# Channel attention and a gated MLP on one core: v's first half split two steps later, turned weights made in three pieces, block 1's v turned within block 0, last block ended by output halves

## The chip, the cores and the metric

The kernel runs on one core of a Trainium2 chip. The metric is device time in microseconds (us). An execution repeats within some 0.1%: the three runs of the kernel before lie between 1318.31 and 1320.58 us.

The engines have two names each: PE is TensorE's matrix product and PEld its weight load, DVE is VectorE, ACT is ScalarE, POOL is GpSimd, SP is SyncE, which here only issues transfers (DMAs).

## The reference

Inputs are q, k and v (2 x 6016 x 256), the weights w_gate, w_val (256 x 1536) and w_out (1536 x 256), and scales, all in fp32.

```python
def _attn_ref(q, k, v, tau):
    qn = q / (np.linalg.norm(q, axis=1, keepdims=True) + 1e-06)
    kn = k / (np.linalg.norm(k, axis=1, keepdims=True) + 1e-06)
    s = kn.transpose(0, 2, 1) @ qn / tau          # 256 x 256 per batch
    ...
    return v @ a                                  # a: softmax of s over its last axis

def _moe_ref(x, w_gate, w_val, w_out, rms_g):
    xn = x / np.sqrt(np.mean(x * x, axis=-1, keepdims=True) + 1e-06) * rms_g
    g = xn @ w_gate
    return (g / (1 + np.exp(-g)) * (xn @ w_val)) @ w_out
```

The attention's output, taken as 12032 rows, is x of the second function.

## The kernel before, in words

**Precision.** Every operand of a large product is split into a high part (a ScalarE copy to a rounded type) and a low part (a subtraction on VectorE or GpSimd). A product is then three matmuls: high by high, high by low, low by high. So each tensor that TensorE reads costs one ScalarE copy and one subtraction, and those have to be done in time.

**Blocks and steps.** The rows of v are cut into 24 blocks of 512 rows (the first and the last of 384). A block has 12 steps, one for each 128 columns f of the hidden layer. (j, f) is step f of block j. Blocks 0 and 1 use plain products (`emit_hidden`, L776 on), with the score products of batch 1 filled in between. From block 2 on, `emit_step` (L710 on) forms the hidden layer with seven products of quarter blocks in place of eight, in a flight of three steps: a step begins with products 7 and 2 of the step that started two steps earlier, continues with products 3 and 6 of the one in the middle, then 5 and 1 of the new one, and ends with product 4 of the oldest, with output products before and behind product 4. `new_state` gives each step one of three PSUM banks with tag u. ScalarE copies products out to t (L739, L744), VectorE adds them (L732, L733), ScalarE applies silu in even steps (L748, L766), VectorE multiplies in odd steps (L751, L760).

**Output.** In odd steps `round_pair` puts down the splits of a finished pair p (p = 0 to 5, steps 2p and 2p+1): first gx (copy L665, subtraction L671 on GpSimd), and in the next odd step gy and, for pairs 2 to 4 from block 4 on (the Strassen pairs), gz. Between the two, in the even step, `run_turned` (L657) forms differences in place in zg, with four VectorE instructions that wait for GpSimd to have read gx's part. The output products of a step (L860) run five steps later. The Strassen pairs need weights s, so, which `build_so` makes in block 3 and 4 in two pieces: piece 0 forms sums on VectorE (L595, L605), piece 1 copies on ScalarE (L611) and subtracts on VectorE (L613). `build_s` does the like for the hidden layer's weights in blocks 1 and 2. Their scratch wk has one buffer, which `post_out`'s sums also use.

**The next x.** While a block's steps run, x of later blocks is made: `load_v`, `move_v` (VectorE transposes into vw, L406; one buffer), `split_v` (ScalarE L390, then L391 on GpSimd, on VectorE for blocks 0 and 1), `emit_x` (TensorE px, L428), `emit_x_squares`, `emit_rr` (GpSimd) and `emit_xn` (ScalarE L469), `emit_xT_move` (VectorE L504, and after its second half 16 transfers on SP, L513), `emit_xT_scale` (ScalarE L523), `emit_xT_parts` (GpSimd L534, L539) and `emit_xT_round` (ScalarE L551, GpSimd L553). Blocks 0 and 1 turn v and x on TensorE instead (`turn_v`, `emit_xT_first`).

**What sets the order.** The order is written out by hand in tables that say which of these parts follows which step: turn0 to turn4 for blocks 0 to 4 and steady for all later ones; their values run behind a step, those of the _mid tables within it and those of the _pre tables before the silu. `of(m, go)` runs go for block j+m. In the tables v0 and v1 are move_v of the two halves, s0 and s1 split_v, x0/q0/r0/n0 and x1/q1/r1/n1 the products, squares, roots and scaling, m0 and m1 the transposes of x, scale, parts, hi and rest what follows. `at(j, f, go)` adds further parts behind a step. Each engine executes its instructions in the order in which they are written. `next_bank` gives blocks 0 and 1 a rotation of four PSUM banks (three of tag u, one of tag q).

The lines that matter most in the tables before:

```python
        steady = {
            1: (scale,),
            3: (hi, v1),
            ...
            11: after(3, vm(0), vs(0)),
        }
```

Of the kernel before, what the change touches and what calls it, by code (L numbers as in the profile page):

```python
# [15 lines left out]
P = 128  # L16
# [3 lines left out]
def kernel(  # L20
# [352 lines left out]

    def turn_v(j, h, psum, tag):

        x = v_t[j].rearrange("p m c r -> p (m c r)")
        v_w[j, h] = psum.tile([P, KC, HN], F32, tag=tag, name=f"pvt_{j}_{h}")
        for c in range(KC):
            for i, t in enumerate(half_tiles(j, h)):
                nc.tensor.transpose(  # L380
                    v_w[j, h][:, c, i * P:(i + 1) * P],
                    x[:, t * C + c * P:t * C + (c + 1) * P], ident,
                )
# [207 lines left out]
    def build_so(k, piece):  # L591
# [14 lines left out]
        else:  # L606
            t = s_tmp.pop(("so", k))[:, 2:].rearrange("p i n -> p (i n)")
            src = (t[:, :3 * P], t[:, 3 * P:])
            hi, lo = ([x[:, k], w[:, 2 * p + 1, P:]] for x, w in zip(so_hl, wo))
            for o, x in zip(hi, src):  # L610
                nc.scalar.activation(out=o, in_=x, func=AF.Copy)  # L611
            for o, x, y in zip(lo, src, hi):
                nc.vector.tensor_tensor(out=o, in0=x, in1=f32(y), op=ALU.subtract)  # L613
# [196 lines left out]
    def out_rows(j):  # L810

        r, mu0 = strided(j)
        return out[r, :].rearrange("(s m) e -> s m e", s=S)[:, mu0:mu0 + A * blocks[j][2], :]
# [32 lines left out]
    def emit_out_turned(j, f):  # L846
# [3 lines left out]
        jobs = G.pop((j, f))  # L850
        todo = [(b, o, w[wi], g[gi], wi + gi) for wis, gi in (((0, 1), 0), ((0,), 1)) for b, o, w, g in jobs for wi in wis]
        half = (len(todo) + 1) // 2

# [44 lines left out]
    def post_store(j):  # L898

        n = blocks[j][2]  # L900
        h = n * P // 2
        w = sums.pop(j)
        ob = v_p.tile([P, A * BT, KC, S], F32, tag="v", name=f"ob_{j}")
        for e in range(2):
            nc.vector.transpose(
                out=ob[:, :A * n, e, :],
                in_=w[:, 2 * e * h:2 * (e + 1) * h].rearrange("p (m s) -> p m s", s=S),
            )
        dst = out_rows(j).rearrange("s m (e i r) -> i s m e r", e=KC, i=A)
        for i in range(A):  # L910
            queue = nc.scalar if i % 2 and j == NB - 1 else nc.sync
            queue.dma_start(
                out=dst[i].rearrange("s m e r -> s (m e) r"),
                in_=ob[S * i:S * (i + 1), :A * n].rearrange("p m e r -> p (m e) r"),
            )
        del o_ps[j]


    with tc.manual_schedule():
# [51 lines left out]
        for h in range(2):  # L971
            turn_v(0, h, ps_gv, "u")
        nc.vector.tensor_scalar(out=mtau, in0=mtau, scalar1=-1.0, scalar2=None, op0=ALU.mult)
# [61 lines left out]
        emit_xT_first(0, 1)  # L1035
        turn_v(1, 0, ps_m, "m")
        add()
# [7 lines left out]
        def at(j, f, go):  # L1045
            extra.setdefault((j, f), []).append(go)
# [41 lines left out]
        at_step = [(2 * p + 2, 2 * p + 3, 2 * p + 4, 2 * p + 4) for p in range(NP - 3)]  # L1088
        at_step += [(8, 9, 10, 12), (13, 14, 15, 16), (16, 18, 19, 20)]
        for i in (2, 3, 0, 1):  # L1090
# [13 lines left out]
        at(STRA - 1, 6, new_so)  # L1104
        for k, (f0, f1) in enumerate(((10, 11), (12, 13), (14, 15))):
            for i, f in enumerate((f0, f1)):
                at(STRA - 1 + f // NF, f % NF, lambda k=k, i=i: build_so(k, i))

# [20 lines left out]
        def vs(h):  # L1129
            return lambda n: split_v(n, h)  # L1130

        def x(h):
            return lambda n: emit_x(n, h)

        def sq(h):
# [8 lines left out]
        def xm(c):  # L1144
            return lambda n: emit_xT_move(n, c)
# [4 lines left out]
        def of(m, go):  # L1150
# [18 lines left out]
        steady = {  # L1169
            1: (scale,),  # L1170
            3: (hi, v1),
# [5 lines left out]
            9: (m0,),  # L1177
            11: after(3, vm(0), vs(0)),
        }
# [3 lines left out]
            **steady,  # L1183
            0: after(1, xm(1)),
            1: (v0, s0),
# [4 lines left out]
        }  # L1190
        turn4_mid = {6: (x0, q0, r0), 8: (x1, q1), 9: (n1,)}
        turn3 = {
            0: after(1, xm(1)),
            3: (v0,),
# [6 lines left out]
            10: (r1,),  # L1201
            11: (m0,),
        }
        turn3_mid = {5: (parts,), 7: (x0, q0, r0), 9: (x1, q1), 11: (n1,)}
        turn2 = {
            **turn3,
            0: after(1, sq(1), rr(1)),
            1: after(1, xn(1), xm(0), xm(1)),
            4: (scale, s0),
# [17 lines left out]
        turn0 = {  # L1227
            0: after(1, vs(0)),
            1: after(1, x(0), sq(0), rr(0)),
            2: after(1, xn(0), lambda n: turn_v(n, 1, ps_m, "m")),  # L1230
            3: after(1, vs(1)),
            4: after(1, x(1), sq(1), rr(1)),
            5: after(1, xn(1)),
            8: (of(1, lambda n: emit_xT_first(n, 0)), v0),
# [36 lines left out]
        post_sums(NB - 1)  # L1271
        for o in owed:
            run = emit_out(*o[1:])
            run(0)
            run(1)
        for e in range(2):
            post_out(NB - 1, e)
        post_store(NB - 1)


# [31 lines left out]
```

## Time and profile before

| | |
|---|---|
| three runs | 1318.31, 1319.4 (median), 1320.58 us |
| the profiled execution | 1320.82 us |
| its span, first to last instruction | 1319.0 us |
| mean granted TensorE clock | 0.993 of 2.4 GHz |
| instructions | 25099, of them 9216 matmuls |

The span lies within the execution; 1.8 us are around it. A matmul's end is modelled, so TensorE's idle time is best read from its waits. A timeline row gives the start, the duration, engine, line, operation, out<-in by the program's names, shape and count, with the idle time of the engine before it and what ended it in brackets.

### The profile page before, as it was taken

Reading aid. Unit: us, or ns where it says so; the run is one execution under the profiler, and the core shown is the slowest. Engines: PE = TensorE matmul, PEld = TensorE weight load, DVE = VectorE, ACT = ScalarE, POOL = GpSimd, SP = SyncE. Lnnn points to the kernel's source line nnn. Section 1 sums busy time; section 2 is a strip of 40 time slices with the busy share of each in tenths; the row PEclk is TensorE's granted clock in tenths of the full one; section 3 lists DMA queues with packets and bytes.
Section 4 is the critical chain, followed back from the end, with each engine's and each line's share of the span. In section 5 each row is a group of like instructions: output and inputs, shape, how many; then the busy total and the mean of one; then the engine's idle time right before and its main releaser. Section 6 shows DMA issues by size and latency. Waiting matters only on the chain.

```text
span 1319.0 us, 25099 instructions
## 1 busy us (share of the span) xinstructions
PE 1274.4 (97%) x9216; PEld 1205.1 (91%) x9216; DVE 965.2 (73%) x1588; ACT 857.3 (65%) x1773; POOL 807.7 (61%) x642
## 2 busy tenths in 40 slices
PE   8989998999999999999999999999999999999997
PEld 7779988998999999999999999999999999999997
DVE  5789687657678767777777777677677687686765
ACT  5566556665766676666666766766766766766653
POOL 0120244765676776776777777777777777776643
PEclk9899999999999999999999999999999999999999
DMA  8868111120211211212202202202202202101101
GB/s 285 286 238 261 40 32 34 22 44 17 43 23 33 40 26 33 37 25 37 33 18 48 33 18 49 33 17 49 33 17 49 34 17 49 29 18 28 17 8 22
DMA packets 226588, 71.77 MB, mean 54 GB/s; under 512 B 189600, under 2 KB 218016, under 8 KB 226464
## 3 DMA queue, kind: packets, MB, share of 16 engines
q1 hardware_dynamic: 224896, 69.97, 23.0%
q8 instruction: 72, 1.18, 0.4%
q14 instruction: 52, 0.43, 0.1%
q10 hardware_dynamic: 1568, 0.20, 0.1%
HBM read 46.40 MB, written 12.32 MB: 45 GB/s over the span
## 4 chain that ended last, share of the span: by engine, by line
PE 53%; DVE 9%; POOL 5%; issue 3%; ACT 2%; SPq 2%; DMA 1%; DVEq 0%; ACTq 0%
PE pu L703 28%; PE po L860 17%; POOL gx L671 5%; PE pq L703 4%; DVE zg L657 4%; PE px L428 4%; ACT gx L665 2%; SPq L513 2%; DVE zg L760 2%; DMA xnT<-xw 1%; DVE zv L732 1%; DVE zg L751 1%; DVE zv L733 0%; DVE zg L732 0%; DVE os L885 0%
## 5 line engine op out<-in xcount | busy, mean ns | idle before, releaser
L703 PE MATMUL pu<-xt,w 128*128 128x256 f32 (+1 forms) x2376 | 415.7, 283 | 18.9 <-DVE zv L732 12.1
L703 PEld LDWEIGHTS pu<-xt,w 128*128 128x128 f32 x2376 | 347.8, 189 | 37.4 <-DVE zv L732 15.7
L703 PE MATMUL pu<-xt,s 128*128 128x256 f32 (+1 forms) x2376 | 372.0, 281 | 3.4 <-ACT t L739 1.4
L703 PEld LDWEIGHTS pu<-xt,s 128*128 128x128 f32 x2376 | 329.0, 189 | 20.0 <-DVE zg L760 5.5
L671 POOL TENSOR_TENSOR gy<-zg,gy 128x512 fp32r<-128x512 f32 (+1 forms) x131 | 170.9, 1305 | 193.7 <-ACT gy L665 160.3
L671 POOL TENSOR_TENSOR gx<-zg,gx 128x512 fp32r<-128x512 f32 (+3 forms) x131 | 202.0, 1542 | 64.4 <-ACT gx L665 55.7
L751 DVE TENSOR_TENSOR zg<-zg,zv 128x768 f32<-128x768 f32 (+1 forms) x132 | 210.8, 1597 | 14.1 <-DVE zv L733 0.5
L744 ACT ACTIVATE t<-pu 128x512 f32<-128x512 f32 (+1 forms) x264 | 156.3, 592 | 87.2 <-PE pu L703 51.0
L860 PE MATMUL po<-gx,w 128*128 128x256 f32 (+3 forms) x972 | 205.2, 330 | 0.7 <-ACT gx L665 0.7
L657 DVE TENSOR_TENSOR zg<-zg 128x256 f32<-128x256 f32 (+1 forms) x240 | 119.5, 498 | 61.8 <-POOL gx L671 55.6
L860 PE MATMUL po<-gy,w 128*128 128x512 f32 (+3 forms) x612 | 163.3, 360 | 0.0
L665 ACT ACTIVATE gx<-zg 128x512 fp32r<-128x512 f32 (+3 forms) x132 | 95.6, 724 | 99.0 <-DVE zg L760 54.8
L860 PEld LDWEIGHTS po<-gx,w 128*128 128x128 f32 x972 | 143.2, 188 | 6.9 <-ACT gx L665 0.8
L732 DVE TENSOR_TENSOR zv<-pu,t 128x512 f32<-128x512 f32 (+1 forms) x132 | 89.8, 680 | 75.7 <-ACT zg L766 36.5
L739 ACT ACTIVATE t<-pu 128x256 f32<-128x256 f32 (+1 forms) x264 | 98.9, 375 | 65.5 <-PE pu L703 64.9
L703 PE MATMUL pq<-xt,w 128*128 128x256 f32 (+1 forms) x792 | 137.2, 281 | 0.0
L732 DVE TENSOR_TENSOR zg<-pu,t 128x512 f32<-128x512 f32 (+1 forms) x132 | 90.3, 684 | 61.3 <-PE pu L703 27.7
L665 ACT ACTIVATE gy<-zg 128x512 fp32r<-128x512 f32 (+1 forms) x132 | 82.7, 626 | 78.6 <-DVE zg L657 63.7
L671 POOL TENSOR_TENSOR gz<-zg,gz 128x512 fp32r<-128x512 f32 (+1 forms) x60 | 118.2, 1969 | 0.0
L703 PEld LDWEIGHTS pq<-xt,w 128*128 128x128 f32 x792 | 112.1, 188 | 0.0
L748 ACT ACTIVATE zg<-zg 128x768 f32<-128x768 f32 (+1 forms) x132 | 109.6, 830 | 0.0
L860 PEld LDWEIGHTS po<-gy,w 128*128 128x128 f32 x612 | 101.1, 188 | 6.2
(138 smaller groups left out, 1977.0 us busy)
## 6 DMA issues: line engine op xcount, KB each, us to landing
v<-in_v_dram SPq DMA_DIRECT2D x84, 128.0 KB, 3.7
xnT<-xw SPq DMA_DIRECT2D x336, 32.0 KB, 1.9
out_dram<-ob SPq DMA_DIRECT2D x84, 128.0 KB, 3.3
raw<-in_q_dram SPq DMA_DIRECT2D x20, 512.0 KB, 5.3
raw<-in_k_dram SPq DMA_DIRECT2D x20, 512.0 KB, 6.5
wraw<-in_moe_w_gate_dram SPq DMA_DIRECT2D x12, 256.0 KB, 3.6
wraw<-in_moe_w_val_dram SPq DMA_DIRECT2D x12, 256.0 KB, 4.1
wraw<-in_moe_w_out_dram SPq DMA_DIRECT2D x12, 256.0 KB, 5.0
```

The source lines that it names most:

```text
L428: nc.tensor.matmul(out=px[:, i, :], lhsT=w[:, c, i * P:(i + 1) * P], rhs=x[:, c, :], start=(i == 0 and c == 0 and m == 0), stop=(c == KC - ...
L513: nc.sync.dma_start(out=x[S * i:S * (i + 1), :, a * n * S:(a + 1) * n * S], in_=w[S * a:S * (a + 1), :, i, :n, :].rearrange("p c t s -> p ...
L657: nc.vector.tensor_tensor(out=z[:, o], in0=z[:, i0], in1=z[:, i1], op=ALU.subtract)
L665: nc.scalar.activation(out=gh, in_=hh, func=AF.Copy)
L671: engine.tensor_tensor(out=gl, in0=hh, in1=f32(gh), op=ALU.subtract)
L703: nc.tensor.matmul(out=out, lhsT=wm[wi], rhs=xm[xi], start=(start and q == 0), stop=(q == 2), skip_group_check=True,)
L732: nc.vector.tensor_tensor(out=z[:, 1:], in0=u, in1=t[:, :2], op=ALU.add)
L739: nc.scalar.activation(out=mt[:, 0], in_=mu[:, 1], func=AF.Copy)
L744: nc.scalar.activation(out=nt[:, 1:], in_=nu, func=AF.Copy)
L748: nc.scalar.activation(out=zg[:, 1:], in_=zg[:, 1:], func=AF.Silu)
L751: nc.vector.tensor_tensor(out=zg[:, 1:], in0=zg[:, 1:], in1=z, op=ALU.mult)
L860: nc.tensor.matmul(out=acc[b][:, o:o + g.shape[-1]], lhsT=w, rhs=g, start=first, stop=True, skip_group_check=True,)
```

## The change

- Steady blocks: the split of v's first half (`split_v`, h = 0) goes from the end of step 11 to the end of step 1 of the next block, ahead of scale. move_v stays at step 11.
- `build_so` has three pieces: sums, copies, subtractions; they stand at steps (3, 8), (3, 11), (4, 0) for the first pair, (4, 0), (4, 1), (4, 2) for the second, (4, 2), (4, 3) and within (4, 4) for the third.
- Block 1's v is turned behind steps 0 and 3 of block 0, into banks of the rotation; split, product and scaling of both halves follow one step later each than before.
- m1 of blocks 4 and 5 goes from step 0 of a block to step 11 of the one before; xn of block 3's second half from (2, 1) to (2, 0); build_s of pair 4 begins at (2, 0) and not (2, 1).
- Last block: the output products of steps 10 and 11 are ordered by output half; each half is summed, transposed and stored by itself, with four transfers on two queues per half in place of four for both.

```diff
-    def turn_v(j, h, psum, tag):
+    def turn_v(j, h):
...
-        v_w[j, h] = psum.tile([P, KC, HN], F32, tag=tag, name=f"pvt_{j}_{h}")
+        v_w[j, h] = next_bank(f"pvt_{j}_{h}").rearrange("p (c n) -> p c n", c=KC)
...
-            t = s_tmp.pop(("so", k))[:, 2:].rearrange("p i n -> p (i n)")
+            t = s_tmp["so", k][:, 2:].rearrange("p i n -> p (i n)")
...
-            for o, x in zip(hi, src):
+            for o, x in zip(hi, src) if piece == 1 else ():
                 nc.scalar.activation(out=o, in_=x, func=AF.Copy)
-            for o, x, y in zip(lo, src, hi):
+            for o, x, y in zip(lo, src, hi) if piece == 2 else ():
                 nc.vector.tensor_tensor(out=o, in0=x, in1=f32(y), op=ALU.subtract)
...
+        if (j, f) >= (NB - 1, NF - 2):
+            todo.sort(key=lambda job: job[0])
...
         for e in range(2):
+            if j == NB - 1:
+                sums[j] = w
+                post_out(j, e)
             nc.vector.transpose(
...
+            if j == NB - 1:
+                dst = out_rows(j)[:, :, e * P:(e + 1) * P].rearrange("s m (i r) -> i s m r", i=A)
+                for i in range(A):
+                    (nc.scalar if i % 2 else nc.sync).dma_start(
+                        out=dst[i], in_=ob[S * i:S * (i + 1), :A * n, e, :]
+                    )
...
-        turn_v(1, 0, ps_m, "m")
...
-        at_step += [(8, 9, 10, 12), (13, 14, 15, 16), (16, 18, 19, 20)]
+        at_step += [(8, 9, 10, 12), (12, 14, 15, 16), (16, 18, 19, 20)]
...
-        for k, (f0, f1) in enumerate(((10, 11), (12, 13), (14, 15))):
-            for i, f in enumerate((f0, f1)):
-                at(STRA - 1 + f // NF, f % NF, lambda k=k, i=i: build_so(k, i))
+        for i, k, f in ((0, 0, 8), (1, 0, 11), (2, 0, 12), (0, 1, 12), (1, 1, 13), (2, 1, 14), (0, 2, 14), (1, 2, 15)):
+            at(STRA - 1 + f // NF, f % NF, lambda k=k, i=i: build_so(k, i))
...
         steady = {
-            1: (scale,),
+            1: (s0, scale),
...
-            11: after(3, vm(0), vs(0)),
+            11: after(3, vm(0)),
...
         turn4 = {
             **steady,
-            0: after(1, xm(1)),
...
-        turn4_mid = {6: (x0, q0, r0), 8: (x1, q1), 9: (n1,)}
+        turn4_mid = {4: (lambda j: build_so(2, 2),), 6: (x0, q0, r0), 8: (x1, q1), 9: (n1,)}
         turn3 = {
-            0: after(1, xm(1)),
...
-            11: (m0,),
+            11: (m0, m1),
...
         turn2 = {
             **turn3,
-            0: after(1, sq(1), rr(1)),
-            1: after(1, xn(1), xm(0), xm(1)),
+            0: after(1, sq(1), rr(1), xn(1)),
+            1: after(1, xm(0), xm(1)),
...
         turn0 = {
-            0: after(1, vs(0)),
-            1: after(1, x(0), sq(0), rr(0)),
-            2: after(1, xn(0), lambda n: turn_v(n, 1, ps_m, "m")),
-            3: after(1, vs(1)),
-            4: after(1, x(1), sq(1), rr(1)),
-            5: after(1, xn(1)),
+            0: after(1, turn(0)),
+            1: after(1, vs(0)),
+            2: after(1, x(0), sq(0), rr(0)),
+            3: after(1, xn(0), turn(1)),
+            4: after(1, vs(1)),
+            5: after(1, x(1), sq(1), rr(1)),
+            6: after(1, xn(1)),
...
-        for o in owed:
-            run = emit_out(*o[1:])
-            run(0)
-            run(1)
-        for e in range(2):
-            post_out(NB - 1, e)
+        owed = [emit_out(*o[1:]) for o in owed]
+        for part in range(2):
+            for go in owed:
+                go(part)
         post_store(NB - 1)
```

## Rows read from the trace of the kernel before

**Rows 1.** The page, part 1: busy us, share of the span, instructions

```profile
PE 1274.4 (97%) x9216; PEld 1205.1 (91%) x9216; DVE 965.2 (73%) x1588; ACT 857.3 (65%) x1773; POOL 807.7 (61%) x642
```

**Rows 2.** TensorE's waits, 340 to 1200 us: by whom; us, times, longest

```profile
PE pu L703 <- DVE zv L732: 12.1, 17, 0.9
```

**Rows 3.** Timeline, VectorE and GpSimd, blocks 17 and 18: start us, us, instruction

```profile
1008.71 1.80 DVE L657 TENSOR_TENSOR zg<-zg 128x256 f32<-128x256 f32 x4 [0.41 <-POOL gx L671]
1016.67 2.88 DVE L657 TENSOR_TENSOR zg<-zg 128x256 f32<-128x256 f32 x4 [1.05 <-POOL gx L671]
1016.59 1.29 POOL L391 TENSOR_TENSOR vt<-vw,vt 128x512 fp32r<-128x512 f32 x1
```

**Rows 4.** Timeline, TensorE entering steps 1 and 3, blocks 18, 22; VectorE

```profile
1016.64 0.52 PE L703 MATMUL pu<-xt,s 128*128 128x256 f32 x3
1025.56 0.51 PE L703 MATMUL pu<-xt,s 128*128 128x256 f32 x3
1215.98 0.52 PE L703 MATMUL pu<-xt,s 128*128 128x256 f32 x3
1223.82 0.51 PE L703 MATMUL pu<-xt,s 128*128 128x256 f32 x3
1216.01 1.80 DVE L657 TENSOR_TENSOR zg<-zg 128x256 f32<-128x256 f32 x4 [1.05 <-POOL gx L671]
```

**Rows 5.** Timeline, ScalarE, GpSimd and VectorE around the new place, block 18

```profile
1014.61 0.62 ACT L390 ACTIVATE vt<-vw 128x512 fp32r<-128x512 f32 x1
1024.33 0.36 ACT L739 ACTIVATE t<-pu 128x256 f32<-128x256 f32 x1
1023.55 1.31 POOL L671 TENSOR_TENSOR gx<-zg,gx 128x512 fp32r<-128x512 f32 x1
1027.03 1.29 POOL L671 TENSOR_TENSOR gy<-zg,gy 128x512 fp32r<-128x512 f32 x1 [2.17 <-ACT gy L665]
1030.36 1.56 POOL L539 TENSOR_TENSOR xp<-xnT,xp 128x256 f32<-128x256 f32 x2
1029.39 0.75 DVE L406 STREAM_TRANSPOSE vw<-v 128x256 f32<-128x256 f32 x2
```

**Rows 6.** Timeline, TensorE's waits around block 0 (idle us and releaser in brackets)

```profile
76.89 0.66 PE L380 MATMUL pvt<-ident,v 128*128 128x128 f32 x4 [1.63 <-DMA v<-in_v_dram]
85.74 2.62 PE L428 MATMUL px<-a,vt 128*128 128x256 f32 x12 [2.24 <-DVE vt L391]
96.81 0.66 PE L380 MATMUL pvt<-ident,v 128*128 128x128 f32 x4 [1.21 <-ACT xn L469]
```

**Rows 7.** Block 0: us; busy PE, PEld, DVE, ACT, POOL; clock; DMA share, GB/s

```profile
77.00:118.40 41.40, 37.95 (x212) 35.42 (x213) 38.01 (x51) 28.27 (x48) 5.58 (x4) 0.96 0.77 232
86.07:89.48 3.41, 3.41 (x16) 3.14 (x15) 3.41 (x6) 2.36 (x8) 0.15 (x1) 0.50 0.14 51
```

**Rows 8.** Timeline, start of block 2: TensorE, GpSimd, ScalarE

```profile
218.14 0.62 PE L703 MATMUL pu<-xt,w 128*128 128x256 f32 x3 [2.21 <-DVE zg L732]
230.84 0.62 PE L703 MATMUL pu<-xt,s 128*128 128x256 f32 x3 [1.39 <-ACT t L739]
211.94 0.72 POOL L457 TENSOR_TENSOR rr<-ss,mhalf 128x2 f32<-128x2 f32 x1
214.08 0.83 ACT L469 ACTIVATE xn<-px,rr 128x256 f32<-128x256 f32 x2
```

**Rows 9.** Timeline, TensorE, blocks 3 and 4

```profile
319.44 0.62 PE L703 MATMUL pu<-xt,w 128*128 128x256 f32 x3 [1.37 <-DVE zg L732]
329.36 0.62 PE L703 MATMUL pu<-xt,w 128*128 128x256 f32 x3 [1.89 <-DVE zg L732]
```

**Rows 10.** Timeline, VectorE and the store's issue at the end

```profile
1311.85 1.02 DVE L894 TENSOR_TENSOR os<-po,os 128x384 f32<-128x384 f32 x2
1313.84 0.89 SPq L912 DMA_DIRECT2D out_dram<-ob  x2
```

**Rows 11.** DMA issues, 1312 to 1320 us: operation xcount, KB each, us to landing

```profile
out_dram<-ob SPq DMA_DIRECT2D x2, 96.0 KB, 3.0
```

More of the change, by code (lines that the diff above doesn't have):

```diff
@@ L908, in post_store @@
             )
+            if j == NB - 1:
[4 more added lines that the diff above has]
+                    )
         dst = out_rows(j).rearrange("s m (e i r) -> i s m e r", e=KC, i=A)
-        for i in range(A):
-            queue = nc.scalar if i % 2 and j == NB - 1 else nc.sync
-            queue.dma_start(
+        for i in range(A if j < NB - 1 else 0):
+            nc.sync.dma_start(
                 out=dst[i].rearrange("s m e r -> s (m e) r"),
@@ L971 @@
         for h in range(2):
-            turn_v(0, h, ps_gv, "u")
+            turn_v(0, h)
         nc.vector.tensor_scalar(out=mtau, in0=mtau, scalar1=-1.0, scalar2=None, op0=ALU.mult)
@@ L1133, in x, with turn @@
             return lambda n: emit_x(n, h)
+        def turn(h):
+            return lambda n: turn_v(n, h)
         def sq(h):
```

## The prediction

> **What bounds the kernel now.** I read the page first: TensorE is busy for 97% of the span, VectorE for 73%, GpSimd for 61% [rows 1]. Such shares are averages, so they only say that an engine that feeds TensorE late costs time, and that nothing else does. Next come TensorE's own waits [rows 2]: from block 4 on one entry stands out, 17 waits of up to 0.9 us for the same VectorE instruction. The count matters: 17 blocks (j = 4 to 20) prepare the v of block j+3 at their step 11. So I read the engines' timelines around one of these waits, at 1016 to 1026 us [rows 3]. The four subtractions of run_turned (L657) take 2.88 us there and 1.80 us one pair earlier. The only thing that differs beside them is GpSimd's subtraction for v's first half (L391, 1.29 us), which starts as they do. The late L657 holds back L732, L732 holds a PSUM bank, and TensorE waits for that bank.
>
> The trace has its own control [rows 4]. Block 21 prepares no v any more (there is no block 24). In step 1 of block 22 L657 takes 1.80 us again, and TensorE has no wait of that kind. From the first product of step 1 to the first of step 3 it needs 1223.82 - 1215.98 = 7.84 us there and 1025.56 - 1016.64 = 8.92 us beside the v work. The difference, 1.08 us, is exactly 2.88 - 1.80. That is the price per block, second-hand delays included.
>
> **Part 1: v's first half split two steps later.** ScalarE's copy and GpSimd's subtraction leave the end of step 11 and go to the end of step 1, ahead of the scaling L523. What is removed: 17 x 1.08 = 18.4 us, all on the path. What the new place costs [rows 5]: on ScalarE the copy (0.62 us) goes in front of L523, behind which the copy L739 queues. L739 ends at 1024.33 + 0.36 = 1024.69; TensorE overwrites what it reads with the first product of step 3, at 1025.56 [rows 4]. Of 0.87 us of slack 0.25 is left: cost nothing, but thin. On GpSimd the subtraction comes right behind gx (1023.55 to 1024.86), and the next thing is gy at 1027.03: 2.17 us are free for 1.29. VectorE's next user of the buffer vw is L406 at 1029.39, long after. No DMA moves. Bounds: nothing lost (18.4), or the copy's whole 0.62 per block on the path (17 x (1.08 - 0.62) = 7.8). I take 18.4, since the slack is measured and the control shows the rest of the chain without further wait.
>
> The Trainium skill, "SBUF — State Buffer", section "Who interferes with whom", says that a VectorE instruction with two SBUF inputs and a GpSimd instruction that reads SBUF exclude each other, the second one blocked until the first is done. By that the whole 1.29 us would be lost and regained, 17 x 1.29 = 21.9 us; the rows give 1.08, and I keep them.
>
> **Part 2: block 1's v turned within block 0.** Before, TensorE waits three times here [rows 6]: 1.63 us for v's load in front of block 0, 2.24 us for VectorE's half of the split, 1.21 us for the PSUM bank m. Together 5.08 us. After the longest its granted clock is 0.50 (1.2 GHz) for 3.41 us [rows 7], which loses half of that, 1.7 us. So 6.8 us are there at most. The change moves the first turn behind step 0 (the load has landed by then), gives both turns banks of the rotation instead of m, and puts one step between turning, splitting and multiplying. But VectorE is nearly full: from 77 to 118.4 us it is busy for 38.01 of 41.40 us, so its stream, which still has to make both splits, can move up by 3.4 us only. TensorE may run ahead of it a little, since it uses weights made two steps earlier. Bounds 3.4 and 6.8; I take 4.1, near VectorE's bound: a shorter wait before each product px remains (about 0.9 and 0.6 us when I lay the two engines' instructions end to end), none of them long enough for the clock to fall, since after the 1.63 us wait it did not fall either. The four transposes per half are moved and not added. Block 0's own turns take the same kind of bank as before: nothing.
>
> **Part 3: start of block 2.** xn(1) of block 3 goes from the end of step 1 to the end of step 0, the first piece of the turned weights of pair 4 likewise. Two waits stand here [rows 8]: 2.21 us for VectorE's L732, queued behind the transposes L504 that wait for xn, and 1.39 us for ScalarE's L739, queued behind a scaling that waits for those transposes' 16 transfers. xn could start once GpSimd's rr is done, at 211.94 + 0.72 = 212.66 instead of 214.08. So transposes, transfers and scaling come 1.4 us earlier, and that is the gain at the second wait, whatever the first becomes. The new order also makes ScalarE wait for rr and delays its copies for TensorE's step 2: I expect a wait of about 1.7 us at the first product of step 2 in place of the 2.21. Bounds 0 and 3.6; I take 1.4.
>
> **Part 4: turned weights in three pieces, and m1 of blocks 4 and 5 one step earlier.** TensorE waits 1.37 and 1.89 us where VectorE's L613 stands in one piece with ScalarE's copies that it needs [rows 9]. With the subtraction a step later VectorE no longer waits for ScalarE, but its work is the same: in steps 0 and 2 of block 4 two pieces now meet (a piece 2 and a piece 0). Of 3.3 us I take 3.0, with 1.5 as the lower end, since VectorE then runs some tenths late. The transposes' 16 transfers are issued on SP about one step earlier, with no other transfer of the loop overtaken; their reader, the scaling, is four steps on: nothing. The earlier transposes add 0.7 us to VectorE in step 11, which step 0 loses.
>
> **Part 5: the end.** VectorE's last four instructions (sums L894 from 1311.85 and transposes L905, up to the issue of the stores at 1313.84: 2.0 us) stay, in the order sum, transpose, sum, transpose; so the first half's four transfers can start about 1.0 us earlier [rows 10]. The last half still starts where all did, but with half the bytes behind it. Landing took 3.0 us for 96 KB [rows 11]. TensorE's reordering only has to finish bank 0 before VectorE gets to L894. I take 1.0 us, bounds 0.3 and 1.5.
>
> The Trainium skill, "DMA: Bandwidth & Descriptors", its table of fixed and variable time, has about 2 us per DMA that do not shrink with size, and only the bytes' own time on top. By that the tail would gain some 0.45 us, as an estimate from that page, in place of 1.0.
>
> **The sum.** 18.4 + 4.1 + 1.4 + 3.0 + 1.0 = 27.9 us. The profiled execution took 1320.82 us (span 1319.0 and 1.8 around it), 1.4 above the median of 1319.4. 1320.82 - 27.9 = 1292.9 there, so 1291.5 for a median run (27.9 off the median). Ends of the terms, not all at once: gains of 22 to 33, 1286 to 1298.
>
> **Rivals.**
> (a) The split finds a new victim. If GpSimd's subtraction slides behind gy of step 3, it stands beside L751, which like L657 reads two SBUF operands, and a wait of the old kind comes back; between nothing and all of the 18.4 us I take half: 27.9 - 9.2 = 18.7, 1300.7. For it: the thin slack on ScalarE. Against: GpSimd executes in program order, and 2.17 us are free in front of gy. 12%. The rule of the Trainium skill's "SBUF — State Buffer", section "Who interferes with whom", allows this case as well as mine.
> (b) Only part 1 and the end pay. In block 0 VectorE is the bound, and the waits of parts 2 to 4 move instead of going: 18.4 + 1.0 = 19.4, 1300.0. For it: 38.01 of 41.40 us. Against: waits of 5.08 us and a fallen clock have to be paid again in places where VectorE has no wait today. 9%.
> (c) The change does not do what it says: L657 is slow for another reason, and part 1 gives nothing: 9.5, 1309.9. Against: the control. 2%.
> (d) Slower. vw is one buffer, and the next thing that VectorE does with it is L406 at 1029.39. If the subtraction ran only behind GpSimd's train of step 3, which ends at 1030.36 + 1.56 = 1031.92 [rows 5], it would end at 1033.2, and L406 would wait 3.8 us with L732 behind it. It decides once the subtraction ends after 1029.39, which is 3.2 us later than the 1026.15 at which it should end. If two thirds of the 3.8 us reach TensorE, 17 x 2.5 = 43 us: 1334. Against: the program order again. 3%.
>
> My forecast has the remaining 74%. The range takes in most of (a) and (b): 1286 to 1300.5. A measurement of this kernel can tell about 0.2%, 2.6 us, from no change. Forecast, (a), (b) and (c) are all faster by more than that; I leave 2% for a mixture that ends within it.
>
> **What would show it.** Right: L657 at 1.8 us in every strassen step, no entry of 17 waits for L732, every block with v work 1.08 us shorter; no granted clock of 0.50 near 86 us; one wait near 216 us, shorter than 2.21; VectorE never waiting for L611; output transfers in two groups, 1 us apart. Wrong: a wait for L739 at step 3's first product, 17 times (part 1's slack was too thin); waits for L391 in block 0 that add up to 5 us (part 2); L732 late in steps 1 to 3 of block 4 (part 4).

## The result, and the profile after

The changed kernel takes 1296.81 us (median of 4 runs, 1295.19 to 1298.8), the kernel before 1319.36 us beside it (median of 4). The ratio is 0.983, with a 95% interval from 0.981 to 0.985. The prediction was 1291.5 us with a range from 1286 to 1300.5, so the sign and the range hold and the middle was 5.3 us too low. The profiled executions differ by 24.9 us (spans 1319.0 and 1294.1), the medians by 22.5, since the execution profiled after was 0.9 us under its median and the one before 1.5 over its own.

The first thing to read is again the page's busy times and TensorE's waits, of the kernel after. Beside [rows 1], TensorE does the same 9216 matmuls and VectorE is busy for 19 us less, though it does the same work.

```profile
PE 1268.4 (98%) x9216; PEld 1202.7 (93%) x9216; DVE 945.9 (73%) x1588; ACT 853.7 (66%) x1773; POOL 806.0 (62%) x642
```

TensorE's waits over the whole span, after (by whom; us in all, times, longest):

```profile
PE s L174 <- DMA raw<-in_k_dram: 5.9, 5, 2.5
PE pu L703 <- ACT t L739: 3.9, 3, 1.8
PE pv L786 <- DVE vt L391: 2.5, 1, 2.5
PE px L428 <- DVE vt L391: 1.6, 1, 1.6
PE pu L703 <- DVE zg L732: 1.3, 1, 1.3
PE pu L703 <- DVE zv L732: 1.3, 2, 1.0
```

The entry of 17 waits for L732 [rows 2] is gone. Where it stood, L657 is as fast in step 1 as in every other step; the group by lines shows it for all 240 instructions (busy us, mean ns), first before and then after:

```profile
L657 DVE TENSOR_TENSOR zg<-zg 128x256 f32<-128x256 f32 (+1 forms) x240 | 119.5, 498 | 61.8 <-POOL gx L671 55.6
L657 DVE TENSOR_TENSOR zg<-zg 128x256 f32<-128x256 f32 (+1 forms) x240 | 101.3, 422 | 61.8 <-POOL gx L671 55.6
```

The timeline of step 1 of one block after, which answers to the late L657 of [rows 3]:

```profile
996.90 1.80 DVE L657 TENSOR_TENSOR zg<-zg 128x256 f32<-128x256 f32 x4 [1.05 <-POOL gx L671]
```

But the list has an entry that the prediction did not have, 2.5 us in one wait of the product pv. Of the three waits for ScalarE's L739 one was forecast, 1.73 us at the first product of step 2 of block 2 ("about 1.7"); the other two, 1.76 and 0.37 us, were not.

**Where the time came from.** The same five matmuls are found in both traces, and the time between them compared. The landmarks are the first product pg of step 11 of block 1, the product 2 (pq) of step 8 of block 2, of step 6 of block 4 and of step 4 of block 21, and the last matmul. Each stretch holds one part of the change. Times in us, from the traces:

| stretch | part | before | after | gain | forecast |
|---|---|---|---|---|---|
| start to block 1, step 11 | 2 | 203.61 | 200.55 | 3.06 | 4.1 |
| to block 2, step 8 | 3 | 36.88 | 36.59 | 0.29 | 1.4 |
| to block 4, step 6 | 4 | 94.46 | 92.00 | 2.46 | 3.0 |
| to block 21, step 4 | 1 | 844.89 | 826.60 | 18.29 | 18.4 |
| to the last matmul | none | 131.52 | 131.73 | -0.21 | 0 |
| to the end | 5 | 7.67 | 6.66 | 1.01 | 1.0 |

Parts 1 and 5 came out as forecast, the other three gave 5.8 us in place of 8.5. The rest of this document asks whether part 1 works for the stated reason, and what took the missing 2.7 us. The last four stretches repeat within about 0.1 us in most executions of the same code, so a single execution is enough to read a part. The first one varies more: the five kernels here with the block 0 of before have 201.57 to 204.54 us, mean 202.8, and seven with that of after 199.04 to 201.78, mean 200.4, so that part 2 is worth 2.5 us over all of them. Experiments for which no interval is given were executed once, and are read by their stretches.

### The profile page after: what moved, and what is told of

The parts are those of the page before. It is cut to its first block, busy times and chain, and to the rows that moved or that the text cites. A ratio compares the mean times of both kernels' runs of the same rounds, so it can differ in the third digit from the quotient of the medians.

```text
span 1294.1 us, 25106 instructions
## 1 busy us (share of the span) xinstructions
PE 1268.4 (98%) x9216; PEld 1202.7 (93%) x9216; DVE 945.9 (73%) x1588; ACT 853.7 (66%) x1773; POOL 806.0 (62%) x642
## 4 chain that ended last, share of the span: by engine, by line
PE 90%; DVE 4%; DMA 2%; issue 1%; SPq 1%; ACT 1%; POOL 1%; DVEq 0%; ACTq 0%; POOLq 0%
PE pu L703 42%; PE po L862 26%; PE pq L703 7%; PE px L428 5%; PE s L174 4%; DMA raw<-in_k_dram 2%; PE po L828 2%; PE pv L786 2%; PE pg L786 2%; SPq L513 1%; DVE wx L122 0%; DVE acc L198 0%; DVE w L137 0%; DVE wo L605 0%; SPq L160 0%
## 5 line engine op out<-in xcount | busy, mean ns | idle before, releaser
L671 POOL TENSOR_TENSOR gy<-zg,gy 128x512 fp32r<-128x512 f32 (+1 forms) x131 | 182.1, 1390 | 176.2 <-ACT gy L665 148.4
L751 DVE TENSOR_TENSOR zg<-zg,zv 128x768 f32<-128x768 f32 (+1 forms) x132 | 202.4, 1533 | 14.1 <-DVE zv L733 0.5
L657 DVE TENSOR_TENSOR zg<-zg 128x256 f32<-128x256 f32 (+1 forms) x240 | 101.3, 422 | 61.8 <-POOL gx L671 55.6
L732 DVE TENSOR_TENSOR zv<-pu,t 128x512 f32<-128x512 f32 (+1 forms) x132 | 89.7, 679 | 74.0 <-ACT zg L766 36.5
L739 ACT ACTIVATE t<-pu 128x256 f32<-128x256 f32 (+1 forms) x264 | 99.0, 375 | 63.9 <-PE pu L703 63.4
L732 DVE TENSOR_TENSOR zg<-pu,t 128x512 f32<-128x512 f32 (+1 forms) x132 | 90.2, 684 | 62.6 <-PE pu L703 27.7
```

The lines of the kernel that those rows point to most:

```text
L657: nc.vector.tensor_tensor(out=z[:, o], in0=z[:, i0], in1=z[:, i1], op=ALU.subtract)
L671: engine.tensor_tensor(out=gl, in0=hh, in1=f32(gh), op=ALU.subtract)
L732: nc.vector.tensor_tensor(out=z[:, 1:], in0=u, in1=t[:, :2], op=ALU.add)
L739: nc.scalar.activation(out=mt[:, 0], in_=mu[:, 1], func=AF.Copy)
L751: nc.vector.tensor_tensor(out=zg[:, 1:], in0=zg[:, 1:], in1=z, op=ALU.mult)
```

## Experiments on the first half's split

**The split alone.** The kernel before, with part 1 and nothing else:

```
-            1: (scale,),
+            1: (s0, scale),
...
-            11: after(3, vm(0), vs(0)),
+            11: after(3, vm(0)),
```

> The kernel before with part 1 alone: in blocks 4 to 20 ScalarE's copy and GpSimd's subtraction of v's first half go from the end of step 11 to the end of step 1, ahead of the scaling. Theory (L657 is slow because L391 runs beside it, 1.08 us in each of 17 blocks): 1319.4 - 18.4 = 1301.0 us, L657 at 1.80 us for its four in every pair, no entry of 17 waits for L732. Rival (L657 is slow for another reason; part 1 pays only together with the other parts): 1319 us, L657 still at 2.88.

Measured 1301.69 us (median of 4; ratio 0.986, 0.983 to 0.988) beside 1319.77. The stretch from block 4 to 21 takes 826.62 us, 18.27 less than before, and L657 has 422 ns. So part 1 stands on its own.

**GpSimd's subtraction alone.** ScalarE's copy stays at step 11 (copy_v and sub_v are the two instructions of split_v):

```
...
-            1: (scale,),
+            1: (after(2, lambda n: sub_v(n, 0))[0], scale),
...
-            11: after(3, vm(0), vs(0)),
+            11: after(3, vm(0), lambda n: copy_v(n, 0)),
```

> The kernel before; ScalarE's copy of v's first half stays at the end of step 11, and GpSimd's subtraction alone goes to the end of step 1, ahead of the scaling. Theory (VectorE and GpSimd get in each other's way): the whole gain, 1301.0 us, L657 at 1.80. Rival (ScalarE's 0.62 us in front of L739 at step 11 is what is late): at most a small part of it, 1311 to 1319 us, with L657 at 1.80 and a wait that stays.

Measured 1300.96 us (ratio 0.986, 0.983 to 0.988), the stretch 826.42 us. The copy in front of L739 costs nothing; GpSimd's instruction is the whole price. In the group by lines (L667 is L657 here, L421 the moved subtraction) VectorE is at its normal time:

```profile
L667 DVE TENSOR_TENSOR zg<-zg 128x256 f32<-128x256 f32 (+1 forms) x240 | 101.2, 422 | 61.8 <-POOL gx L681 55.6
L421 POOL TENSOR_TENSOR vt<-vw,vt 128x512 fp32r<-128x512 f32 x17 | 22.5, 1325 | 0.0
```

**Twice the subtraction.** The same suspect, doubled, in the kernel before:

```
...
+        if h == 0 and j > STRA + 2:
+            nc.gpsimd.tensor_tensor(out=hl[1], in0=w, in1=f32(hl[0]), op=ALU.subtract)
```

> The kernel before; GpSimd makes the subtraction of v's first half twice in a row at the end of step 11 (same result), 17 times. Theory (each GpSimd instruction that reads SBUF holds off a VectorE instruction that reads two SBUF operands for as long as it runs): L657's four take about 2.88 + 1.1 = 4.0 us and the kernel 1319 + 17 x 1.1 = 1338 us. Rival (only the start of L657 collides, or the two share the access at a fixed rate that the second one finds free): L657 stays near 2.9 and the time near 1320.

Measured 1337.52 us; the stretch takes 863.39 us, 18.5 more than before, the mirror image of part 1. The timeline of one step 1 (L661 is L657 here, L421 the second subtraction):

```profile
1029.50 1.29 POOL L391 TENSOR_TENSOR vt<-vw,vt 128x512 fp32r<-128x512 f32 x1
1030.87 1.35 POOL L421 TENSOR_TENSOR vt<-vw,vt 128x512 fp32r<-128x512 f32 x1
...
1029.58 3.84 DVE L661 TENSOR_TENSOR zg<-zg 128x256 f32<-128x256 f32 x4 [1.04 <-POOL gx L675]
```

L661's four take 3.84 us, after 1.80 without a neighbour and 2.88 with one. Each subtraction costs VectorE about 1 us, and the second finds nothing free.

**A fill in its place.** GpSimd writes the same tile at the same place and reads nothing; the low part of the first half of v is left out:

```
-        split(v_w.pop((j, h))[:, :, :m], [x[:, :, :m] for x in vT[j, h]], engine)
...
+        if h == 0 and j > STRA + 2:
+            nc.scalar.activation(out=hl[0], in_=w, func=AF.Copy)
+            nc.gpsimd.memset(f32(hl[1]), 0.0)
+        else:
+            split(w, hl, engine)
```

> The kernel before; at the end of step 11 of blocks 4 to 20 GpSimd's subtraction of v's first half is replaced by filling its output with zeros, an instruction of the same engine at the same place that writes the same tile and reads nothing. It leaves out the low part of the first half of v. Theory (GpSimd's reads are what holds VectorE's second operand off): L657 at 1.80 us, about 1301 us. Rival (any access of GpSimd to SBUF, writing too, holds it off): L657 longer than 1.80 by about the fill's duration, 1310 to 1319 us.

Measured 1303.03 us, the stretch 826.21 us. The fill and L657 (L663 here) run at the same time, and neither is slower for it:

```profile
1001.91 0.53 POOL L421 MEMSET vt<- 128x512 f32 x1
...
1002.01 1.80 DVE L663 TENSOR_TENSOR zg<-zg 128x256 f32<-128x256 f32 x4 [1.04 <-POOL gx L677]
```

So it is what GpSimd reads, not where it works or that it writes, that holds off a VectorE instruction with two SBUF inputs (the fill is shorter than the subtraction, 0.53 us for 1.29, but none of its 0.53 us shows in L657). The Trainium skill says the same in "SBUF — State Buffer", section "Who interferes with whom" (with a GpSimd instruction that reads SBUF such an instruction contends, with one that only writes it does not); the two traces agree with it. That the two inputs matter shows in the changed kernel: VectorE's L732, which has one input in SBUF and one in PSUM, runs 122 times between 340 and 1200 us with at least half of its time beside a GpSimd subtraction, and takes 0.68 to 0.69 us each time; the other 88 take 0.65 to 0.69.

## Experiments on block 0, the start of block 2, and blocks 3 and 4

**The wait that was not forecast (part 2).** Timeline of the changed kernel, TensorE's two waits in block 0 and VectorE's split:

```profile
89.70 1.57 PE L428 MATMUL px<-a,vt 128*128 128x256 f32 x11 [1.59 <-DVE vt L391]
...
108.48 1.29 PE L786 MATMUL pv<-xt,w 128*128 128x384 f32 x6 [2.47 <-DVE vt L391]
...
107.18 0.55 DVE L671 TENSOR_TENSOR gy<-hh,gy 128x384 fp32r<-128x384 f32 x1
107.65 0.68 DVE L391 TENSOR_TENSOR vt<-pvt,vt 128x512 fp32r<-128x512 f32 x1
```

The first was forecast (0.9 us; it is 1.59). The second is a product pv of block 0, which has no use for block 1's v. It waits for a bank: every fourth tile of the rotation is the one q bank, the second turned v is the rotation's twelfth tile, and pv of step 5 its sixteenth, the next to get q. The turned v gives q up only when VectorE, busy without a gap, comes to L391. The experiment takes the bank of the rotation away from it:

```
-            3: after(1, xn(0), turn(1)),
-            4: after(1, vs(1)),
-            5: after(1, x(1), sq(1), rr(1)),
-            6: after(1, xn(1)),
+            3: after(1, xn(0)),
+            4: after(1, turn(1)),
+            5: after(1, vs(1)),
+            6: after(1, x(1), sq(1), rr(1)),
+            7: after(1, xn(1)),
...
+        if j == 0 or h == 0:
...
+        else:
+            v_w[j, h] = ps_m.tile([P, KC, HN], F32, tag="m", name=f"pvt_{j}_{h}")
```

> The changed kernel; block 1's second turned v gets the PSUM bank m again in place of one of the rotation. The four transposes go one step later (end of step 4), so that m is free by then, and split, product and norm of that half one step later with them. Theory (the 2.47 us that TensorE waits at 108.48 us are there because the turned v sits in the one q bank of the rotation until VectorE's split): that wait goes, the products px of steps 6 and later start 1.4 us (VectorE's idle time behind that wait, 0.62 + 0.80) to 2.5 us earlier than in the changed kernel, up to the start of block 2, so a span near 1292. Rival (VectorE, full in this stretch, is the bound): a wait of the same size appears at another of its instructions (L391 in front of px, or L800), and the later steps start no earlier than 0.5 us before those of the changed kernel.

Measured 1291.17 us, span 1289.4. The wait for pv is gone and none came in its place; TensorE's waits for the split, after that edit, are one (L431 is L428, L394 is L391):

```profile
PE px L431 <- DVE vt L394: 1.6, 1, 1.6
```

From the first product pg of block 0 to step 11 of block 1 it needs 123.35 us; the seven kernels here that keep the bank need 126.04 to 127.59 (126.04 in the profiled changed kernel). That is 2.7 us, a little more than the wait itself. The longer values are those in which TensorE's clock fell behind this wait, as in this window of one of them (columns as in [rows 7]; the kernel with the later scaling, below):

```profile
108.60:112.00 3.40, 3.40 (x16) 3.40 (x15) 2.92 (x5) 0.53 (x1) 0.00 (x0) 0.50 1.10 159
```

The edit changes bank and step together, so which of the two would do alone is not told apart.

**Part 3 undone.**

```
-            0: after(1, sq(1), rr(1), xn(1)),
-            1: after(1, xm(0), xm(1)),
+            0: after(1, sq(1), rr(1)),
+            1: after(1, xn(1), xm(0), xm(1)),
...
-        at_step += [(8, 9, 10, 12), (12, 14, 15, 16), (16, 18, 19, 20)]
+        at_step += [(8, 9, 10, 12), (13, 14, 15, 16), (16, 18, 19, 20)]
```

> The changed kernel with part 3 undone: xn(1) of block 3 at the end of step 1 of block 2 again, and the first piece of the turned weights of pair 4 one step later. Theory (part 3 only exchanged waits; by the two traces its whole effect is 0.28 us): the two waits near 212 and 227 us come back as 2.2 us for L732 and 1.4 us for L739, and the span stays within 0.5 us of the changed kernel's over this stretch. Rival (the forecast of 1.4 us was right and something else in the changed kernel took it): 1.4 us longer over this stretch.

Measured 1295.5 us. The stretch takes 36.92 us, 0.33 more than with part 3. The waits are 2.2 us for L732 and 2.2 for L739, the second longer than the 1.39 of [rows 8]: TensorE's clock did not fall behind the first one this time, and TensorE, earlier, only waited longer. So part 3 exchanged waits. What it exchanged them against is to be seen in the timeline of the changed kernel, ScalarE and SP's queue:

```profile
210.08 0.84 ACT L469 ACTIVATE xn<-px,rr 128x256 f32<-128x256 f32 x2 [1.59 <-POOL rr L457]
210.81 1.08 ACT L840 ACTIVATE ob<-po 128x512 f32<-128x512 f32 x2
211.76 0.40 ACT L739 ACTIVATE t<-pu 128x256 f32<-128x256 f32 x1
...
211.92 0.36 SPq L841 DMA_DIRECT2D out_dram<-ob  x1
212.47 10.81 SPq L513 DMA_DIRECT2D xnT<-xw  x16
...
224.79 1.34 ACT L523 ACTIVATE xnT<-xnT,g_sb 128x512 f32<-128x512 f32 x2 [1.97 <-DMA xnT<-xw]
227.07 0.36 ACT L739 ACTIVATE t<-pu 128x256 f32<-128x256 f32 x1
```

ScalarE stands still for rr, then does L840 ahead of L739: that makes TensorE's wait of 1.73 us at 212.22. Then SP needs 10.81 us to issue 16 transfers one after the other, and ScalarE waits for the last one with L739 queued behind: the wait of 1.76 us at 227.49. In the kernel with part 3 undone the train takes 10.19 us and L523 starts 24.56 us after the landmark in block 1 (224.19 - 199.63); here it starts 24.24 us after it (224.79 - 200.55):

```profile
212.47 10.19 SPq L513 DMA_DIRECT2D xnT<-xw  x16
...
224.19 1.33 ACT L523 ACTIVATE xnT<-xnT,g_sb 128x512 f32<-128x512 f32 x2 [2.39 <-DMA xnT<-xw]
```

The 0.3 us between the two is all that part 3 gained.

Two things took the rest. First, rr was late. The piece of weights that part 3 moved (L571, two SBUF inputs) now runs beside GpSimd's L453 ahead of rr, which took 0.67 us in place of 0.22: the conflict of part 1 the other way round, with GpSimd as the one that waits. The timelines after (two rows) and before (one row):

```profile
207.88 1.29 DVE L571 TENSOR_TENSOR wk<-w,w 128x512 f32<-128x512 f32 x2
208.58 0.67 POOL L453 TENSOR_SCALAR ss<-ss 128x2 f32<-128x2 f32 x1 [1.01 <-ACT xn L444]
...
211.64 0.22 POOL L453 TENSOR_SCALAR ss<-ss 128x2 f32<-128x2 f32 x1 [1.01 <-ACT xn L444]
```

Second, the train took 0.62 us longer, because one of its issues took 1.20 us (duration in ns, least, median and longest):

```profile
L513 SPq DMA_DIRECT2D xnT<-xw x16: 591/595/1203, 212.5 to 222.7; - x16
```

The store L841 (512 KB) is issued directly ahead of the train here, and 3.65 us ahead of it in the kernel before and with part 3 undone. It did not hold back the train's start, which comes 0.16 us behind the end of the transposes (0.12 with part 3 undone). Whether it makes that one issue long is not shown: the next experiment has the same order and a train of 10.21 us.

**Block 1's last outputs behind step 1's products.**

```
-                if j == WINO and f < 2:
+                if j == WINO and f < 1:
```

> The changed kernel; at step 1 of block 2 the output products of block 1's last step, with ScalarE's two copies of them (L840, 1.08 us), go behind the step's own products in place of ahead of them. Nothing is added. Theory (TensorE's wait of 1.73 us at 212.22 is the 1.59 us that ScalarE waits for GpSimd's rr plus L840's 1.08 in front of L739): the wait shrinks to 0.5 us or less, since L739 comes 1.08 us earlier and TensorE has 1.28 us of work more in front of the product that needs it; 1.2 us less by step 2 of block 2, and the half-clock stretch at 213 us goes. Rival (what is missing is only moved to the next wait for L739 at 227 us): that wait grows by as much as the first shrinks, and nothing is left at step 6 of block 2.

A miss, and the rival in its stronger form: 1298.03 us, the stretch 39.52 us, 2.9 longer. The first wait shrank to 0.4 us, and TensorE came to step 3 2.5 us earlier; but TensorE's waits for L739 now have one of 4.2 us:

```profile
PE pu L703 <- ACT t L739: 4.9, 3, 4.2
```

The timeline of SP's queue there, the store first and then the 16 transfers:

```profile
211.15 0.36 SPq L841 DMA_DIRECT2D out_dram<-ob  x1
211.70 10.21 SPq L513 DMA_DIRECT2D xnT<-xw  x16
```

The transposes had ended at 210.79 there, but the store, which has to wait for the later L840, goes first. L523 starts 24.41 us after the landmark (223.45 - 199.04), 0.17 later than in the changed kernel. Whatever TensorE gains ahead of the train, it loses behind it, and here more than that, since its clock is at 0.50 for 6.83 us from 225.5 on.

**The scaling later.**

```
-            4: (scale, s0),
+            4: (s0,),
...
+        turn2_mid = {**turn3_mid, 5: (scale, parts)}
...
```

> The changed kernel; in block 2 the scaling of block 3's transposed rows (L523) goes from the end of step 4 to the middle of step 5, behind ScalarE's copies L739 and L744 of that step. Theory (the 16 transfers on SP's queue, 10.2 to 10.8 us from the first issue to the last, set when L523 starts; TensorE waits at 227.49 us only because L739 is queued behind L523, and so what part 3 gained at the first wait was lost at the second): the wait of 1.76 us goes, and 1.7 us remain gained at step 8 of block 2 and later. Rival (the work behind L523, the parts on GpSimd and L551, is what is late, not L739's place in the queue): a wait of 1 us or more comes back in steps 6 to 8.

Measured 1295.16 us; the stretch takes 34.57 us, 2.0 less than in the changed kernel, and the wait at 227 us does not come back. So it was L739's place in ScalarE's queue behind the scaling that cost, not the transfers' data.

**Both together.**

```
-                if j == WINO and f < 2:
+                if j == WINO and f < 1:
...
-            4: (scale, s0),
+            4: (s0,),
...
+        turn2_mid = {**turn3_mid, 5: (scale, parts)}
...
```

> The kernel with the scaling one half step later, and with block 1's last output products behind the products of step 1 of block 2 as well. Behind step 1 alone these products gained 2.5 - 1.5 = 1.0 us at step 2 and 2.5 us at step 3, and lost more than that at the wait for L739 behind the transfers. Theory (the transfers were the only reason for the loss): nothing is lost any more, and the span over this stretch is 1.0 to 2.5 us shorter than with the later scaling alone. Rival (the transfers, issued 0.7 us later because the output's store stands in front of them on SP's queue, make another reader late): a wait for L551 or for L739 in steps 5 to 8 that takes 1 us or more of it.

Measured 1292.57 us; the stretch 34.05 us, 0.5 less than with the scaling alone. The rival holds for the most part: a wait of 1.4 us for L739 comes back, because the store L841 is issued on SP in front of the transfers (211.83 and 212.37 us there; the transposes had ended at 211.46) and waits for L840, which is now later. The scaling then waits for the train again, with step 6's L739 behind it.

**Piece 0 of the first pair (part 4).** After, TensorE waits at 296 us where it did not before. VectorE, GpSimd and TensorE there:

```profile
288.31 1.83 DVE L595 TENSOR_TENSOR wo<-w,w 128x512 f32<-128x512 f32 x1
290.18 5.19 DVE L605 TENSOR_TENSOR wo<-wo 128x128 f32<-128x128 f32 x4
295.29 0.68 DVE L732 TENSOR_TENSOR zv<-pu,t 128x512 f32<-128x512 f32 x1
...
288.29 1.30 POOL L671 TENSOR_TENSOR gx<-zg,gx 128x512 fp32r<-128x512 f32 x1
289.55 1.75 POOL L391 TENSOR_TENSOR vt<-vw,vt 128x512 fp32r<-128x512 f32 x1
291.31 2.61 POOL L553 TENSOR_TENSOR xt<-xp,xt 128x512 fp32r<-128x512 f32 x2
293.88 1.34 POOL L671 TENSOR_TENSOR gy<-zg,gy 128x512 fp32r<-128x512 f32 x1
...
296.02 0.62 PE L703 MATMUL pu<-xt,w 128*128 128x256 f32 x3 [0.99 <-DVE zv L732]
```

Five small VectorE instructions take 7.0 us; before the change, at step 10, they took 1.8. GpSimd runs five instructions in the same time, as if each of VectorE's had to let one of them pass. It is the conflict that part 1 removes, made anew by part 4, which put piece 0 at step 8. The experiment puts it back:

```
-        for i, k, f in ((0, 0, 8), (1, 0, 11), (2, 0, 12), (0, 1, 12), (1, 1, 13), (2, 1, 14), (0, 2, 14), (1, 2, 15)):
+        for i, k, f in ((0, 0, 10), (1, 0, 11), (2, 0, 12), (0, 1, 12), (1, 1, 13), (2, 1, 14), (0, 2, 14), (1, 2, 15)):
```

> The changed kernel; piece 0 of the first pair's turned output weights goes from the end of step 8 of block 3 to the end of step 10, where it stood before. Theory (L595 and L605 take 7.0 us at step 8, in place of 1.8, because four instructions of GpSimd that read SBUF run beside them, and L732 behind them makes TensorE wait 0.99 us): L595 0.75 and L605 1.0 us, no wait at 296, 1.0 us less over this stretch. Rival (VectorE is late there anyway, or the work is as slow at step 10): a wait of 0.5 us or more there or in the next two steps.

Measured 1294.34 us; the stretch from block 2 to block 4 takes 90.73 us, 1.27 less than in the changed kernel, with no wait at 296:

```profile
297.04 0.75 DVE L595 TENSOR_TENSOR wo<-w,w 128x512 f32<-128x512 f32 x1
297.83 1.02 DVE L605 TENSOR_TENSOR wo<-wo 128x128 f32<-128x128 f32 x4
```

**The last stores whole again (part 5).** The sums and matmuls stay in the new order:

```
-            if j == NB - 1:
...
-                for i in range(A):
-                    (nc.scalar if i % 2 else nc.sync).dma_start(
...
-        for i in range(A if j < NB - 1 else 0):
-            nc.sync.dma_start(
+        for i in range(A):
+            (nc.scalar if i % 2 and j == NB - 1 else nc.sync).dma_start(
```

> The changed kernel, with the last block's four stores whole again, behind both transposes; the order of the matmuls, sums and transposes at the end stays that of the changed kernel. Theory (the gain at the end is that half of the bytes start about 1 us earlier): the time from the start of the last matmul to the end, 6.66 us in the changed kernel, is 7.6 us again, as before the change (7.67). Rival (the earlier sums, by the order of TensorE's matmuls, gave it): 6.7 us.

The last stretch takes 7.64 us (1296.25 - 1288.61), against 6.66. The gain is the stores'. The DMA issues of the changed kernel, which answer to [rows 11], show how: half the bytes land in 2.0 us in place of 3.0, and the second half starts where all four did before.

```profile
out_dram<-ob SPq DMA_DIRECT2D x4, 48.0 KB, 2.0
```

**A better version.** The bank, piece 0, the later scaling and the later outputs together, and block 1's store issued behind the 16 transfers:

```
+            def put():
...
+            if j == 0:
+                put()
+            else:
+                at(2, 1, put)
```

> The changed kernel with four of these edits together: the second turned v in bank m (2.7 us by its trace), piece 0 of the first pair at step 10 (1.3 us), the later scaling with block 1's last output products behind step 1's own (2.6 us), and a new one: block 1's store is issued on SP behind the 16 transfers, not ahead of them. Theory (the edits lie in stretches of their own and add up; the store held the transfers back by 0.9 us, from which L523 gains and the wait of 1.61 us for L739 behind it loses as much): 2.7 + 1.3 + 2.6 + 0.8 = 7.4 us, 1289.4 us. Rival (the store is not what the transfers waited for, or the stretches push each other's waits along): 6.6 us or less, 1290.2 us or more, with the wait near 225 us still 1.6 us.

Measured 1288.70 us (median of 5, 1286.29 to 1291.26; ratio to before 0.976, 0.974 to 0.978), the best here. From block 0's first pg to block 1's step 11 it takes 123.34 us (2.7 less than the changed kernel), then 32.78 us (3.8 less) and 90.77 us (1.2 less): 7.7 us where 7.4 were forecast. TensorE's three waits for L739 are 0.9 us in all (L742 here):

```profile
PE pu L706 <- ACT t L742: 0.9, 3, 0.4
```

The timeline of SP's queue after that edit:

```profile
210.01 10.21 SPq L516 DMA_DIRECT2D xnT<-xw  x16
220.32 0.53 SPq L845 DMA_DIRECT2D out_dram<-ob  x1
```

Counted from the landmark in block 1, the train starts 0.79 us earlier than with the store in front of it (210.01 - 198.15 against 212.37 - 199.72) and is 0.53 us shorter (10.21 for 10.74); TensorE's wait of 1.4 us behind it is 0.2 us.

## Why the prediction was right, and where it was not

**Part 1, right in size and reason.** The control in block 22 gave 1.08 us per block, and 17 x 1.08 = 18.4 against 18.29. Undoing nothing else, moving the subtraction alone, doubling it and replacing it by a fill all agree with the stated cause. The Trainium skill's rule in "SBUF — State Buffer", section "Who interferes with whom", taken as a wait for the whole of L391, gave 21.9 us; the trace gives less, 18.29. The slack on ScalarE, 0.25 us by the forecast, was enough in all 17 blocks. In block 18 L739 ends 0.34 us ahead of the first product of step 3:

```profile
1004.01 0.36 ACT L739 ACTIVATE t<-pu 128x256 f32<-128x256 f32 x1
1004.71 0.51 PE L703 MATMUL pu<-xt,s 128*128 128x256 f32 x3
```

One new wait for L739 appeared, 0.37 us in block 7. It is not that of the thin slack: it stands at step 4, behind the softmax of the second batch, which shares ScalarE there. Rivals (a), (c) and (d) fall: there is no entry of many waits, L657 is fast, and L406 waits for nothing.

**Part 2, one term missing.** The step that failed is "gives both turns banks of the rotation instead of m", which was costed at nothing. It cost 2.5 us: by the rows the wait is for the one single bank of the rotation, which VectorE releases late. The other waits went as laid out, one of them larger (1.59 for 0.9). In the rows, 6.8 us of waits and lost clock before became 1.59 + 2.47 = 4.06 us of waits, with the clock at 1.00 from the first pg to the second of them. The gain of 3.06 us (2.5 over all kernels) lies below the lower bound of 3.4. Without the bank it is 5.8 us, inside the bounds, and above the 4.1 that I took "near VectorE's bound". VectorE was full, but not the bound: TensorE worked ahead of it.

**Part 3, the step "that is the gain at the second wait" failed.** The gain at the second wait was to be what xn gains, 1.4 us. Counted from the landmark in block 1, xn starts 9.53 us behind it in place of 10.47, so it gained 0.94 us: rr, which was taken as unchanged, ended 0.45 us later because of its new neighbour L571. The train starts 0.90 us earlier but takes 0.62 us longer, and L523 starts 24.24 us behind the landmark in place of 24.53. That leaves 0.29 us, the gain of the stretch. The prediction priced the 16 transfers as a fixed delay, and did not ask beside what GpSimd's rr would run. The wait at step 2 came as forecast (1.73 us for about 1.7), but a gain at the first wait is lost at the second as long as the train sets it.

**Part 4, right but for one step.** "Of 3.3 us I take 3.0" missed the new place of piece 0, whose neighbours on GpSimd were not looked up; 1.27 us were lost there, and the rest of the part gave more than I took (2.46 + 1.27 = 3.7). That 2.46 came near 3.0 is luck: two errors of opposite sign.

**Part 5** came as worked out: 1.01 us of 1.0. By the Trainium skill's "DMA: Bandwidth & Descriptors", section "Anatomy of one DMA — SWDGE (gpsimd) path", with 2 us per DMA that do not shrink, the estimate was 0.45 us; the landing time fell by 1.0 us for half the bytes, so the trace differs from it. These transfers are issued on SP and ScalarE, and that section is on those of GpSimd.

Rival (b) is part of the truth: in each of parts 2 to 4 some of the gain moved to a new wait, and 2.7 us of the 8.5 forecast are missing. The measured time stays inside the range because the range was drawn to take in most of that rival. Of the 5.3 us to 1291.5 the traces account for 3.0 (24.9 us gained for 27.9); the rest is that the profiled execution before was slower than its median and the one after faster.

## What to carry to other kernels

A VectorE instruction with two SBUF inputs and a GpSimd instruction that reads SBUF should not be scheduled beside each other; when one is moved away from such a neighbour, look up the new neighbours of everything else that moves, on both engines: a VectorE instruction that moves can make a GpSimd instruction late as well. A tile that borrows a bank from a rotation is held until its slowest reader is done, so count which later tile gets that bank. Before pricing an earlier start, find the serial train behind it (here 16 transfers on one queue) and what is queued in front of it and behind its waiter.

## What was not expected of the hardware

Four 128x128 VectorE instructions, 1.02 us by themselves, took 5.19 us beside a row of GpSimd subtractions: a short instruction of this kind loses far more than its own length. At the start of block 2 SP issued 16 transfers of 32 KB in 10.2 to 10.8 us in every kernel here, about 0.64 us each, while the data of one landed 1.9 us after its issue (median). So it is the sixteen issues one after the other that make the train long, more than the time one transfer takes. TensorE's clock fell to 0.50 behind the 2.47 us wait in three of the seven kernels that have it and stayed at 1.0 in the other four, at the same place in the same code.
